# Gated mix of linear attention and a mixer MLP: LayerNorm 1 takes its sums from TensorE and ScalarE, and loads, readers and the last chunk are reordered

## The chip, the core and the metric

The kernel runs on one core of a Trainium2 chip. A core has five engines, each with its own in-order queue of instructions: TensorE (PE in the profile) for matrix products, with weight loads shown apart as PEld; VectorE (DVE) and ScalarE (ACT) for elementwise work; GpSimd (POOL); and SyncE (SP), which here only issues DMA transfers. Products land in PSUM, everything else lives in SBUF. The metric is the device time of one execution, in microseconds (us), as the median of several runs.

## The reference

One input `x` of 2048 rows by 640 columns (bf16) goes through two branches, which a gate mixes row by row.

```python
g = sigmoid((x * gate_w).sum(-1))                 # one gate value for each row

# branch A: linear attention, 32 heads of 20 columns
q, k, v = split(x @ wqkv)
phi = lambda t: where(t > 0, t + 1, exp(t)) + 1e-6
kv  = sum over rows of phi(k)^T v ;  z = sum over rows of phi(k)     # for each head
a   = (phi(q) kv / (phi(q) z + 1e-6)) @ wo

# branch B: mixer MLP
h  = gelu(layernorm(x) @ w1)                      # LayerNorm 1
hs = (four column groups of h, shifted by 1, -1, 2, -2 rows) @ w2
x1 = x + hs
b  = x1 + gelu(layernorm(x1) @ w3) @ w4           # LayerNorm 2

out = g * a + (1 - g) * b
```

A LayerNorm here needs, for each row, the mean and the variance over 640 columns, and no weights.

## The kernel before

The 2048 rows are 16 chunks of 128. The order of all instructions is written out by hand, engine by engine; there is no scheduler. Four PSUM tiles `PP[0..3]` of 128 x 1024 fp32 are handed out by `alloc` and given back by `release`, first in, first out. TensorE waits where a tile that it is given has not yet been read by its last reader.

The stages, by the span of the profiled execution:

- **Start** (to 11 us). `x` is loaded in natural layout (`x_sb`) and, transposed by DMA, as `xT`. Chunks 0 to 2 are transposed on TensorE instead (`x_tr`, L295) and copied out of PSUM by two VectorE copies (L297, L298). The K weights come in five pieces on ScalarE's DMA queue, followed there by the Q weights `wq` (L176); all other loads are on SyncE's queue in program order. Column 640 of the K weights is the gate vector (L305), so that the K product of a chunk also gives the gate's row sums in PSUM column 640.
- **K stage** (11 to 45 us). For each chunk `c`: ten matmuls (`k_mm`, L262) into a PSUM tile; then `k_post`, which calls `phi`: Exp on ScalarE (L256), a min and add on VectorE in SBUF (L257), and a `scalar_tensor_tensor` on VectorE that reads the product in PSUM again (L258). Then a one-column Exp of the gate column on ScalarE (`ey`, L267), and only then `release`. One step of G = x^T phi(K) for chunk c-3 follows on TensorE (`g_unit`, L272, two matmuls), and from chunk 5 on one task of LayerNorm 1.
- **LayerNorm 1 tasks** (`ln1_tasks`): for a chunk two `bn_stats` (L210, L213) and a `bn_aggr` (L214) on VectorE give mean and variance; for each pair of chunks GpSimd makes the reciprocal root by `pow` (L218, L219); VectorE applies it (`ln1_apply`, L226), and SyncE transposes the result into `lnxT` by DMA (L228). In the Q stage three tasks are taken for each Q step.
- **Q stage** (45 to 85 us). Ten Q steps of ten matmuls (L369), each with `phi` over 1024 columns, and five or six G steps behind each; the column sums `z` are made after steps 2 and 4 (`z_rows`, `z_cols`). Then the remaining G steps, the gate (L388 to L390), and four VectorE copies that pack the last 32 columns of each group of `w1` into `w1x` (L396).
- **w1, attention matrices** (85 to 112 us, L404 and others), **w2** (112 to 134 us, L537), **w3 and w4 with the mix** (134 us to the end: L552, L578, L616, L610). The very last chunk is done in two column parts, 512 and 128 columns of one PSUM tile (L610), each with its final VectorE operation (L588) and its output DMA.

Of the kernel before, what the change touches and what calls it, by code (L numbers as in the profile page):

```python
# [16 lines left out]
def kernel(  # L17
# [27 lines left out]
    KW = D + 1  # L45
# [65 lines left out]
    ey = sb("ey", NCH, F32)  # L111
# [64 lines left out]
    aq.dma_start(wq, rows(A_wqkv, 0, D))  # L176
    sp.dma_start(wv, rows(A_wqkv, 2 * D, 3 * D))
    sp.dma_start(w1, rows(B_w1, 0, D))
# [6 lines left out]

    nc.gpsimd.memset(ones32[:], 1.0)
# [36 lines left out]

    def ln1_apply(c):
        lx = lnxs[c % NLX]
        nc.vector.tensor_scalar(lx[:], x_sb[:, c, :], mv1[:, c, 0:1], rs1[:, c:c + 1],  # L226
                                op0=ALU.subtract, op1=ALU.mult)
# [25 lines left out]
    def phi(dst, src, n):  # L253
        e = eb[ecnt[0] % NE]
        ecnt[0] += 1
        act(e[:, 0:n], src, ACT.Exp)  # L256
        nc.vector.tensor_scalar(e[:, 0:n], e[:, 0:n], 1.0, 1e-6, op0=ALU.min, op1=ALU.add)  # L257
# [7 lines left out]
    def k_post(c, p):  # L265
        phi(pk[:, c, :], PP[p][:, 0:D], D)
        act(ey[:, c:c + 1], PP[p][:, D:D + 1], ACT.Exp, scale=-1.0)  # L267
# [25 lines left out]
    def x_tr(c, b):  # L293
# [3 lines left out]
        nc.vector.tensor_copy(xT[:, 0:2, c * P:(c + 1) * P], v[:, 0:2])  # L297
        nc.vector.tensor_copy(xT[:, 2:5, c * P:(c + 1) * P], v[:, 2:5])  # L298
# [5 lines left out]
    for dc in range(DC):  # L304
        nc.vector.tensor_copy(wkg[:, dc, D:D + 1], tb[1][:, dc:dc + 1])  # L305
# [360 lines left out]
```

## Time and profile before

| what | value |
|---|---|
| time, median of 3 runs | 281.55 us (281.39 to 282.06) |
| the profiled execution's own time | 280.44 us |
| its span in the profile | 278.7 us |
| granted TensorE clock | 0.998 of full speed |
| busy PE, DVE, ACT, POOL | 95%, 48%, 35%, 11% of the span |
| DMA | 23.95 MB, mean 86 GB/s |

The span is what the profiler sees from the first to the last instruction; 1.7 us of the profiled execution lie around it. In rows of the timeline the columns are start (us from the span's start), duration, engine, line, operation, output <- input, count, and in brackets how long the engine stood idle before it and which instruction ended that wait. Two consecutive matmuls overlap in the records, so the distance from start to start, not the duration, is what a matmul costs TensorE.

### The profile page before, as it was taken

The numbers are of one execution on the slowest core, as the hardware profiler recorded it, in microseconds if no ns is written. First come the engines' busy times: TensorE is split into PE (matmuls) and PEld (weight loads), VectorE is DVE, ScalarE is ACT, GpSimd is POOL, SyncE is SP. The second block draws the span as 40 slices with busy tenths as digits, with TensorE's granted clock in tenths as the row PEclk, the third lists the DMA queues.
The fourth block names the chain that finished last, engine by engine and source line by source line (L and its number), as shares of the span: only waits on it lengthen the run. The fifth ranks groups of instructions, "written<-read, shape, count | busy, mean of one in ns | idle before, by whom it ended". The sixth has DMA issues, their size and how long they took to land.

```text
span 278.7 us, 4206 instructions
## 1 busy us (share of the span) xinstructions
PE 263.7 (95%) x1698; PEld 135.9 (49%) x1698; DVE 132.7 (48%) x266; ACT 98.4 (35%) x129; POOL 31.9 (11%) x98
## 2 busy tenths in 40 slices
PE   5868888999998999999999999999999999999994
PEld 2434444555553644555444445555544444555552
DVE  2257778989974606599990012432310001233242
ACT  1133433333324476133598550220215445022020
POOL 4000101111210000044685000000000000000000
PEclk9999999999999999999999999999999999999999
DMA  7999960412452026995274100010010000001001
GB/s 205 260 274 282 271 146 2 87 24 45 81 46 52 0 51 210 356 289 79 51 115 95 23 2 24 24 49 24 26 47 0 0 2 0 24 26 47 27 24 48
DMA packets 42119, 23.95 MB, mean 86 GB/s; under 512 B 30963, under 2 KB 41331, under 8 KB 42099
## 3 DMA queue, kind: packets, MB, share of 16 engines
q1 hardware_dynamic: 40690, 22.04, 33.6%
q10 hardware_dynamic: 1376, 1.64, 1.9%
q8 instruction: 13, 0.21, 0.3%
q14 instruction: 8, 0.06, 0.1%
q0 software_dynamic: 32, 0.00, 0.0%
HBM read 12.86 MB, written 3.44 MB: 58 GB/s over the span
## 4 chain that ended last, share of the span: by engine, by line
PE 81%; DVE 10%; ACT 5%; issue 1%; DMA 1%; POOL 0%; DVEq 0%
PE pp L616 19%; PE pp L552 19%; PE pp L404 8%; PE pp L578 8%; PE pp L537 8%; PE pp L369 7%; DVE RPK L258 5%; ACT eb L256 4%; PE pp L272 4%; DVE eb L257 2%; PE pp L561 2%; PE pp L610 1%; PE pp L262 1%; DMA RXH<-in_A_x_dram 1%; PE pp L601 1%
## 5 line engine op out<-in xcount | busy, mean ns | idle before, releaser
L616 PE MATMUL pp<-RB,RXH 128*128 128x512 bf16 (+1 forms) x390 | 54.4, 299 | 0.0
L552 PE MATMUL pp<-lnxT,RA 128*128 128x512 bf16 x240 | 52.1, 379 | 0.0
L616 PEld LDWEIGHTS <-RXH 128*128 128x128 bf16 x390 | 29.7, 98 | 24.2 <-issue 2.1
L552 PEld LDWEIGHTS <-RA 128*128 128x128 bf16 x240 | 23.4, 98 | 28.1
L554 ACT ACTIVATE RXH<-pp 128x1024 bf16<-128x1024 f32 x24 | 24.2, 1019 | 26.7 <-PE pp L552 26.7
L581 ACT ACTIVATE RXH<-pp,g_all 128x640 f32<-128x640 f32 x16 | 12.7, 794 | 54.9 <-PE pp L578 54.9
L256 ACT ACTIVATE eb<-pp 128x640 bf16<-128x640 f32 (+1 forms) x26 | 21.4, 823 | 24.6 <-PE pp L369 20.0
L262 PE MATMUL pp<-RA,RXT 128*128 128x512 bf16 (+1 forms) x160 | 24.3, 299 | 6.1 <-ACT ey L267 5.3
L272 PE MATMUL pp<-RPK,RXH 128*128 128x512 bf16 (+1 forms) x160 | 25.6, 299 | 1.5 <-DVE RPK L258 1.1
L583 DVE SCALAR_TENSOR_TENSOR RPK<-RPK,omg,RXH 128x640 f32<-128x640 f32 x8 | 7.1, 884 | 36.5 <-ACT RXH L581 36.5
L369 PE MATMUL pp<-RXT,RA 128*128 128x512 bf16 x100 | 23.2, 379 | 0.5 <-ACT ey L267 0.3
L578 PE MATMUL pp<-Mp,pqT 128*128 128x512 bf16 (+1 forms) x160 | 23.1, 299 | 0.0
L537 PE MATMUL pp<-w,RXH 128*128 128x512 bf16 (+1 forms) x160 | 21.9, 299 | 0.0
L262 PEld LDWEIGHTS <-RXT 128*128 128x128 bf16 x160 | 12.7, 97 | 17.2 <-issue 7.0
L583 DVE SCALAR_TENSOR_TENSOR RXT<-RXT,omg,RXH 128x640 f32<-128x640 f32 x8 | 7.1, 884 | 24.6 <-ACT RXH L581 24.6
L272 PEld LDWEIGHTS <-RXH 128*128 128x128 bf16 x160 | 12.8, 98 | 12.2 <-issue 1.7
L218 POOL TENSOR_SCALAR ve<-mv 128x1 f32<-128x1 f32 (+1 forms) x24 | 5.6, 235 | 113.0 <-DVE mv L214 112.4
L404 PE MATMUL pp<-lnxT,RB 128*128 128x512 bf16 x80 | 18.3, 379 | 0.0
L578 PEld LDWEIGHTS <-pqT 128*128 128x128 bf16 x160 | 12.2, 98 | 10.0 <-issue 0.8
L537 PEld LDWEIGHTS <-RXH 128*128 128x128 bf16 x160 | 12.3, 98 | 9.6
L588 DVE SCALAR_TENSOR_TENSOR RXH<-pp,omg,RPK 128x640 bf16<-128x640 f32 (+2 forms) x9 | 7.3, 809 | 20.1 <-PE pp L616 17.2
L588 DVE SCALAR_TENSOR_TENSOR RXH<-pp,omg,RXT 128x640 bf16<-128x640 f32 x8 | 7.1, 884 | 19.8 <-PE pp L616 19.8
(102 smaller groups left out, 247.4 us busy)
## 6 DMA issues: line engine op xcount, KB each, us to landing
out_dram<-RXH SPq DMA_DIRECT2D x15, 160.0 KB, 1.8
RA<-in_B_w_dram SPq DMA_DIRECT2D x5, 432.0 KB, 6.9
RXH<-in_A_x_dram SPq DMA_DIRECT2D x2, 640.0 KB, 5.1
RB<-in_B_w_dram SPq DMA_DIRECT2D x1, 1120.0 KB
RB<-in_B_w_dram SPq DMA_DIRECT2D x1, 960.0 KB, 13.0
RA<-in_A_wqkv_dram ACTq DMA_DIRECT2D x5, 160.0 KB, 4.1
RA<-in_A_wqkv_dram ACTq DMA_DIRECT2D x1, 800.0 KB, 8.5
RA<-in_A_wqkv_dram SPq DMA_DIRECT2D x1, 800.0 KB, 6.8
```

The lines of the kernel that those rows point to most:

```text
L256: act(e[:, 0:n], src, ACT.Exp)
L262: mm(PP[p][:, n0:n1], lhsT=xT[:, dc, c * P:(c + 1) * P], rhs=wkg[:, dc, n0:n1], start=(dc == 0), stop=(dc == DC - 1))
L272: mm(PP[p][:, n0:n1], lhsT=x_sb[:, c, i * P:(i + 1) * P], rhs=pk[:, c, n0:n1], start=(c == 0), stop=(c == NCH - 1))
L369: mm(PP[p][:, tt * 512:(tt + 1) * 512], lhsT=wqp[:, dc, j], rhs=xT[:, dc, t0:t0 + 512], start=(dc == 0), stop=(dc == DC - 1))
L404: mm(PP[p][:, tt * 512:(tt + 1) * 512], lhsT=lh, rhs=lnxT[:, dc, t0:t0 + 512], start=(dc == 0), stop=(dc == DC - 1))
L537: mm(PP[p][:, n0:n1], lhsT=hsT[:, fc, 2 + c * P:2 + (c + 1) * P], rhs=w2[:, fc, n0:n1], start=(fc == 0), stop=(fc == DC - 1))
L552: mm(PP[p][:, k * 512:(k + 1) * 512], lhsT=w3[:, dc, (fc + k) * P:(fc + k + 1) * P], rhs=lnxT[:, dc, t * 512:(t + 1) * 512], start=(dc == ...
L554: act(h2T[:, t % 2, fc:fc + 2, :], PP[p][:].rearrange("p (k s) -> p k s", k=2), ACT.Gelu_apprx_tanh)
L578: mm(PP[p][:, n0:n1], lhsT=pqT[:, j, c * P:(c + 1) * P], rhs=Mp[:, j, n0:n1], start=(j == 0), stop=(j == DC - 1))
L583: nc.vector.scalar_tensor_tensor(x1(c), x1(c), omg[:, c:c + 1], ga, op0=ALU.mult, op1=ALU.add)
L588: nc.vector.scalar_tensor_tensor(oc[:, n0:n1], PP[p][:, n0:n1], omg[:, c:c + 1], x1(c)[:, n0:n1], op0=ALU.mult, op1=ALU.add)
L616: mm(PP[p][:, n0:n1], lhsT=h2T[:, k, fc, cc], rhs=w4[:, fc, n0:n1], start=False, stop=(fc == NF - 1))
```

## The change

- The K weights get a second extra column, of ones (`KW = D + 2`), set by GpSimd. PSUM column 641 of a chunk's K product is then the row sum of `x`.
- In `k_post`, ScalarE copies both extra columns (gate and row sum) to `ym` directly behind the Exp of `phi`; the Exp for the gate is taken once for all chunks behind the Q stage.
- LayerNorm 1: ScalarE squares a chunk with a running sum (`ln1_sq`); after each fourth chunk GpSimd makes mean, variance and reciprocal root for four chunks. `bn_stats` and `bn_aggr` of LayerNorm 1 are gone. One `ln1_sq` is taken at every second chunk from 4 on in the K stage and at each Q step; `ln1_apply` is taken at chunks 12 to 15, at Q steps 3, 4, 7 and 8 (two each), and four behind the Q stage.
- Loads: the K weight pieces 0, 1, 2, 4 stay on ScalarE's queue, piece 3 goes to SyncE's behind the first three chunks; the transposed loads are cut 1, 1, 2, 2, 3, 4 chunks instead of 1, 2, 2, 4, 4; `wq` goes to SyncE's queue behind all of `x`, then `w1`, then `wv`.
- The `w1x` packing moves from VectorE behind the Q stage to GpSimd, ahead of all its LayerNorm work.
- `x_tr`: the copy out of PSUM is split between VectorE (3 of 5 blocks) and ScalarE (2 of 5). Its place among the first K matmuls is moved.
- `z_rows`: a small transpose comes ahead of the column sums instead of behind.
- The last chunk's two column parts get a PSUM tile each.

```diff
-    KW = D + 1
+    KW = D + 2
...
-    for dc in range(DC):
-        aq.dma_start(wkg[:, dc, 0:D], A_wqkv[dc * P:(dc + 1) * P, D:2 * D])
+    def load_wk(q, dc):
+        q.dma_start(wkg[:, dc, 0:D], A_wqkv[dc * P:(dc + 1) * P, D:2 * D])
+    for dc in (0, 1, 2, 4):
+        load_wk(aq, dc)
     load_x(0, 1)
     load_x(1, 2)
     load_x(2, 3)
+    load_wk(sp, 3)
     load_xT(3, 4)
+    load_xT(4, 5)
     load_x(3, 4)
-    load_xT(4, 6)
+    load_xT(5, 7)
     load_x(4, 6)
...
-    aq.dma_start(wq, rows(A_wqkv, 0, D))
+    sp.dma_start(wq, rows(A_wqkv, 0, D))
+    sp.dma_start(w1, rows(B_w1, 0, D))
     sp.dma_start(wv, rows(A_wqkv, 2 * D, 3 * D))
-    sp.dma_start(w1, rows(B_w1, 0, D))
...
+    for dc in range(DC):
+        nc.gpsimd.memset(wkg[:, dc, D + 1:D + 2], 1.0)
...
+    for g in range(4):
+        nc.gpsimd.tensor_copy(w1x4[:, :, g, :], w1g[:, :, g, P:CG])
...
+    def ln1_sq(c):
+        act(junk[:], x_sb[:, c, :], ACT.Square, accum_out=sq[:, c:c + 1])
+        if c % 4 == 3:
+            g = slice(c - 3, c + 1)
+            nc.gpsimd.tensor_scalar(me[:, g], ym[:, g, 1], 1.0 / D, None, op0=ALU.mult)
+            nc.gpsimd.tensor_tensor(ve[:, g], me[:, g], me[:, g], op=ALU.mult)
+            nc.gpsimd.tensor_scalar(sq[:, g], sq[:, g], 1.0 / D, EPS, op0=ALU.mult, op1=ALU.add)
+            nc.gpsimd.tensor_tensor(ve[:, g], sq[:, g], ve[:, g], op=ALU.subtract)
+            nc.gpsimd.tensor_tensor(rs1[:, g], ve[:, g], nhalf[:], op=ALU.pow)
...
-    def phi(dst, src, n):
+    def phi(dst, src, n, extra=None):
         e = eb[ecnt[0] % NE]
         ecnt[0] += 1
         act(e[:, 0:n], src, ACT.Exp)
+        if extra is not None:
+            act(extra[0], extra[1], ACT.Copy)
...
     def k_post(c, p):
-        phi(pk[:, c, :], PP[p][:, 0:D], D)
-        act(ey[:, c:c + 1], PP[p][:, D:D + 1], ACT.Exp, scale=-1.0)
+        phi(pk[:, c, :], PP[p][:, 0:D], D, (ym[:, c, :], PP[p][:, D:D + 2]))
         release(p)
...
-        nc.vector.tensor_copy(xT[:, 0:2, c * P:(c + 1) * P], v[:, 0:2])
-        nc.vector.tensor_copy(xT[:, 2:5, c * P:(c + 1) * P], v[:, 2:5])
+        nc.vector.tensor_copy(xT[:, 0:3, c * P:(c + 1) * P], v[:, 0:3])
+        act(xT[:, 3:5, c * P:(c + 1) * P], v[:, 3:5], ACT.Copy)
...
         g_unit(0, c - 3)
-        if c >= 5:
-            pop(ln1_tasks, 1)
+        if c % 2 == 0:
+            pop(ln1_s)
+        if c >= 12:
+            pop(ln1_a)
...
-            pop(ln1_tasks, 3)
+            pop(ln1_s)
+            if n_ in (3, 4, 7, 8):
+                pop(ln1_a, 2)
...
-    for g in range(4):
-        nc.vector.tensor_copy(w1x4[:, :, g, :], w1g[:, :, g, P:CG])
...
         ps = [alloc(), alloc()]
+        if last:
+            ps.append(alloc())
...
-                for (n0, n1) in COLS:
+                for (p, (n0, n1)) in zip((ps[1], ps[2]), COLS):
```

What this does to the order on the engines is shown at three places. In these rows `pp` is a PSUM tile, `eb` a buffer of Exp results, `RXH` holds `x_sb`, `RXT` holds `xT`, `RPK` holds phi(K), `RB` holds `w1`; `[waits DVE_49]` means that the instruction waits for a count of finished VectorE instructions. Line numbers of the changed kernel are up to 16 higher than before.

ScalarE in the K stage before the change, chunks 3 to 5:

```order
L256 ACTIVATE eb_70<-pp_114 128x640 [waits PE_49]
L267 ACTIVATE ey<-pp_114 128x1 [waits DVE_49]
L256 ACTIVATE eb_71<-pp_112 128x640 [waits PE_49]
L267 ACTIVATE ey<-pp_112 128x1 [waits DVE_49]
L256 ACTIVATE eb_72<-pp_113 128x640 [waits PE_49]
L267 ACTIVATE ey<-pp_113 128x1 [waits DVE_49]
```

ScalarE in the K stage after the change, chunks 3 to 5:

```order
L268 ACTIVATE eb_70<-pp_116 128x640 [waits DVE_49,PE_49]
L270 ACTIVATE ym<-pp_116 128x2
L268 ACTIVATE eb_71<-pp_114 128x640 [waits DVE_49,PE_49]
L270 ACTIVATE ym<-pp_114 128x2
L239 ACTIVATE junk,sq<-RXH 128x640 [waits DMAHW1_49]
L268 ACTIVATE eb_72<-pp_115 128x640 [waits DVE_49,PE_49]
L270 ACTIVATE ym<-pp_115 128x2
```

The small reader of the extra columns no longer waits for VectorE; the Exp now waits for VectorE itself, since one of three `eb` buffers is used again, and the first Square stands between chunks 4 and 5.

GpSimd behind its set-up work, before the change (the first LayerNorm pair):

```order
L201 MEMSET RXH 128x5x4
L202 MEMSET RXH 128x5x4
L218 TENSOR_SCALAR ve<-mv_94 128x2 [waits DVE_49]
L219 TENSOR_TENSOR rs_97<-ve,nhalf 128x2 [waits Pool_49]
L218 TENSOR_SCALAR ve<-mv_94 128x2 [waits DVE_49]
```

The same place after the change:

```order
L211 MEMSET RXH 128x5x4
L212 MEMSET RXH 128x5x4
L216 COPY w1x<-RB 128x5x32 [waits DMAHW4_49]
L216 COPY w1x<-RB 128x5x32 x3
L242 TENSOR_SCALAR me<-ym 128x4 [waits Activation_49]
L243 TENSOR_TENSOR ve<-me 128x4 [waits Pool_49]
L244 TENSOR_SCALAR sq<-sq 128x4 [waits Activation_49]
L245 TENSOR_TENSOR ve<-sq,ve 128x4 [waits Pool_49]
L246 TENSOR_TENSOR rs_99<-ve,nhalf 128x4 [waits Pool_49]
```

The four copies wait for the DMA that brings `w1`, and the first four chunks' LayerNorm values stand behind them in GpSimd's queue.

VectorE at chunks 12 to 14 of the K stage, after the change:

```order
L272 SCALAR_TENSOR_TENSOR RPK<-pp_116,eb_70 128x640 [waits DVE_49,PE_49,Activation_49]
L250 TENSOR_SCALAR lnxs_73<-RXH,me,rs_99 128x640 [waits DMAHW1_49,Pool_49]
L271 TENSOR_SCALAR eb_71<-eb_71 128x640 [waits Activation_49]
L272 SCALAR_TENSOR_TENSOR RPK<-pp_114,eb_71 128x640 [waits DVE_49,PE_49,Activation_49]
L250 TENSOR_SCALAR lnxs_74<-RXH,me,rs_99 128x640 [waits DMAHW3_49]
L271 TENSOR_SCALAR eb_72<-eb_72 128x640 [waits Activation_49]
```

The first `ln1_apply` (L250) waits for GpSimd, and the second half of `phi` of chunks 13, 14 and 15 stands behind it on VectorE.

More of the change, by code (lines that the diff above doesn't have):

```diff
@@ L334, in z_rows @@
     def z_rows():
+        p = alloc()
+        nc.tensor.transpose(PP[p][:, 0:64].bitcast(BF16), mask4[:], ident[:])
+        act(E4[:], PP[p][:, 0:64].bitcast(BF16), ACT.Copy)
+        release(p)
         p = alloc()
@@ L382 @@
         g_unit(*gq.pop(0))
-        pop(ln1_tasks, 1)
-    while ln1_tasks:
-        pop(ln1_tasks)
-    nc.vector.tensor_scalar(g_all[:], ey[:], 1.0, None, op0=ALU.add)
+    assert not ln1_s
+    pop(ln1_a, 4)
+    assert not ln1_a
+    act(g_all[:], ym[:, :, 0], ACT.Exp, scale=-1.0)
+    nc.vector.tensor_scalar(g_all[:], g_all[:], 1.0, None, op0=ALU.add)
     nc.vector.reciprocal(g_all[:], g_all[:])
     nc.vector.tensor_scalar(omg[:], g_all[:], -1.0, 1.0, op0=ALU.mult, op1=ALU.add)
-    w1g = w1.rearrange("p k (g c) -> p k g c", c=CG)
-    w1x4 = w1x.rearrange("p k (g c) -> p k g c", g=4)
-    for g in range(4):
-        nc.vector.tensor_copy(w1x4[:, :, g, :], w1g[:, :, g, P:CG])
     def w1_unit(half, fc):
@@ L600, in w4_units @@
                 q = slice(FT * k, FT * (k + 1))
-                mm(PP[ps[k]][:, n0:n1], lhsT=h2x[q, cc], rhs=w4[q, NF, n0:n1], start=True, stop=False,
+                p = ps[2] if last and k == 1 and n0 else ps[k]
+                mm(PP[p][:, n0:n1], lhsT=h2x[q, cc], rhs=w4[q, NF, n0:n1], start=True, stop=False,
                    tile_position=(FT * k, 0))
```

44 lines of the change are left out of this document (16 added, 28 removed).

## The prediction

> **What bounds the kernel now.** I read the busy shares first, then the busy time by stage, then the waits in order of size, then the timeline at the places that the waits name. The stages are marked by the first Exp (11.2), the first G step alone (45.0), the first w1 product (85.1).
>
> ```profile
> PE 263.7 (95%) x1698; PEld 135.9 (49%) x1698; DVE 132.7 (48%) x266; ACT 98.4 (35%) x129; POOL 31.9 (11%) x98
> 11.20:45.00 33.80, 26.71 (x174) 14.30 (x173) 23.62 (x48) 12.21 (x32) 1.92 (x4) 1.00 0.90 221
> 45.00:85.10 40.10, 39.16 (x263) 21.44 (x262) 35.53 (x84) 14.45 (x18) 6.01 (x12) 1.00 0.31 51
> 133.90:278.70 144.80, 141.02 (x889) 70.98 (x886) 41.01 (x67) 48.17 (x54) 13.48 (x40) 1.00 0.13 31
> ```
>
> The reader is to see that TensorE (first busy column behind the length) is the bound everywhere but in the K stage, where it is busy 26.7 of 33.8 us, VectorE 23.6 and ScalarE 12.2. No engine is full there, so a chain of waits must set the pace.
>
> ```profile
> ACT ey L267 <- DVE RPK L258: 21.6, 16, 1.7
> PE pp L262 <- ACT ey L267: 5.3, 12, 1.7
> PE pp L272 <- DVE RPK L258: 1.1, 1, 1.1
> PE pp L404 <- DVE w1x L396: 0.8, 1, 0.8
> PE pp L610 <- DVE RXH L588: 0.8, 1, 0.8
> ```
>
> Each of 16 chunks makes ScalarE wait, 21.6 us in all, for the last VectorE operation of `phi` before the one-column `ey`, and TensorE waits 12 times for that `ey`. The timeline shows the ring.
>
> ```profile
> 17.65 1.52 PE L262 MATMUL pp<-RA,RXT 128*128 128x512 bf16 x10 [0.29 <-ACT ey L267]
> 18.23 0.33 DVE L257 TENSOR_SCALAR eb<-eb 128x640 bf16<-128x640 bf16 x1 [0.83 <-ACT eb L256]
> 18.66 0.82 DVE L258 SCALAR_TENSOR_TENSOR RPK<-pp,eb 128x640 bf16<-128x640 f32 x1
> 19.01 0.43 PE L272 MATMUL pp<-RPK,RXH 128*128 128x512 bf16 x2
> 19.51 0.17 ACT L267 ACTIVATE ey<-pp 128x1 f32<-128x1 f32 x1 [1.32 <-DVE RPK L258]
> 19.74 1.52 PE L262 MATMUL pp<-RA,RXT 128*128 128x512 bf16 x10 [0.29 <-ACT ey L267]
> ```
>
> Exp (what VectorE waits for at 18.23), min, product, `ey`, and only then the next Exp: the next chunk's matmuls come 19.74 - 17.65 = 2.09 us later. ScalarE's queue is in order, so `ey`, not its 0.17 us, holds back the next Exp. TensorE itself needs 19.01 - 17.65 = 1.36 us for ten K matmuls, and 0.27 for a G step (8 G matmuls, four steps, in 46.08 - 45.00 below): 1.63 us a chunk.
>
> **The change: the K stage.** The copy of both extra columns now stands directly behind Exp and waits for nothing on VectorE, so the ring is cut. What remains for a chunk: TensorE 1.63; VectorE 0.43 from min to product and 0.82 for the product, 1.27 with the gaps, 1.70 where an `ln1_apply` of 0.43 is added; ScalarE 0.70 + 0.17, and a Square at every second chunk. Square has no row; the nearest are Exp from PSUM at 0.70 and the 640-column ACTIVATE below at 0.92. I take 0.80, since it reads SBUF like the dearer one but without per-row operands: two chunks then cost ScalarE 2 x 0.87 + 0.80 = 2.54, against TensorE's 3.26. TensorE becomes the bound. `bn_stats` leaving VectorE is worth nothing on top: VectorE had 10 us idle here. The wider K matmul adds one column of 641 and is neglected.
>
> ```profile
> 11.21 0.70 ACT L256 ACTIVATE eb<-pp 128x640 bf16<-128x640 f32 x1 [4.56 <-PE pp L262]
> 15.56 1.52 PE L262 MATMUL pp<-RA,RXT 128*128 128x512 bf16 x10 [1.66 <-ACT ey L267]
> 41.03 2.32 PE L369 MATMUL pp<-RXT,RA 128*128 128x512 bf16 x10 [0.29 <-ACT ey L267]
> 45.00 1.25 PE L272 MATMUL pp<-RPK,RXH 128*128 128x512 bf16 x8 [1.11 <-DVE RPK L258]
> 46.08 2.32 PE L369 MATMUL pp<-RXT,RA 128*128 128x512 bf16 x10
> 48.24 1.52 PE L272 MATMUL pp<-RPK,RXH 128*128 128x512 bf16 x10
> L518 ACT ACTIVATE lnxs<-RPK,nb,rs 128x640 bf16<-128x640 f32 x8 | 7.3, 915 | 1.8 <-POOL nb L222 1.3 <-DMA lnxT<-lnxs 0.5
> L226 DVE TENSOR_SCALAR lnxs<-RXH,mv,rs 128x640 bf16<-128x640 bf16 x16 | 6.2, 431 | 1.1 <-POOL rs L219 1.1
> ```
>
> With the first Exp at 11.21 as before, chunk 4's matmuls (15.56) need the tile of chunk 1: 11.21 + 0.74, then two rounds of 1.26 on VectorE, is 14.5. Twelve chunks at 1.63 put the first Q step at 14.5 + 19.6 = 34.1 (before 41.03). A Q step is 48.24 - 46.08 = 2.16, six G steps 1.63, so the second Q step starts at 37.9 (before 46.08): **8.2 us** gained if nothing new waits. The waits of 1.66 and 1.11 in these rows are in that.
>
> **The new wait.** GpSimd's four `w1x` copies wait for `w1`; the LayerNorm values of chunks 0 to 3 are queued behind them; `ln1_apply(0)` waits for those, and behind it on VectorE stand `phi` of chunks 13 to 15, for which TensorE waits.
>
> ```profile
> 22.39 0.51 SPq L177 DMA_DIRECT2D RA<-in_A_wqkv_dram  x1
> RA<-in_A_wqkv_dram SPq DMA_DIRECT2D x1, 800.0 KB, 6.8
> 22.93 0.52 SPq L178 DMA_DIRECT2D RB<-in_B_w_dram  x1
> RB<-in_B_w_dram SPq DMA_DIRECT2D x1, 800.0 KB, 9.7
> 30.66 0.25 POOL L218 TENSOR_SCALAR ve<-mv 128x2 f32<-128x2 f32 x1 [25.94 <-DVE mv L214]
> 30.98 0.72 POOL L219 TENSOR_TENSOR rs<-ve,nhalf 128x2 f32<-128x2 f32 x1
> L191 POOL TENSOR_SCALAR_AFFINE_SELECT bmask<-bmask 128x120 f32<-128x120 f32 x1 | 0.3, 332 | 0.1
> ```
>
> Before, `wv` landed at 22.39 + 6.8 = 29.2 and `w1` behind it at 22.93 + 9.7 = 32.6. In the new order one 800 KB matrix fewer lies ahead of `w1` (`wq` moves from ahead of most of `x` to just ahead of it, `wv` behind it), which these two rows price at 3.4 us: `w1` lands between 29.2 and 32.6. I take 30.0, near the lower end, since what counts ahead of it is bytes. GpSimd then needs four copies at about 0.35 (nearest row: 0.33 for 120 columns, these have 160) and five small operations, four at 0.31 from start to start and one `pow` of 0.75: 3.4 us, so `ln1_apply(0)` starts at a = 33.4. `phi(12)` is done at 31.0, so VectorE stands for 2.4 us. The first Q step needs `phi(13)`'s tile, at a + 1.7 = 35.1 instead of 34.1; the G step of chunk 15 needs `phi(15)` at a + 5.1 = 38.5, where TensorE would be at 37.8. TensorE loses 1.0 + 0.7 = **1.7 us**; generally a - 31.7 where that is positive. At the ends: 0.9 for `w1` at 29.2, nothing for 28.3 or earlier, 4.3 for 32.6.
>
> By the Trainium skill ("SBUF — State Buffer", Who interferes with whom), VectorE's two-port modes and GpSimd lock each other out for a whole instruction, which speaks against four copies on GpSimd beside `phi`. The copies would wait out at most a min of 0.33 each, an estimate of 1.3 us more on the loss; no row of this trace has such a pair, and I leave it to the range.
>
> **Loads and start.** `wq` now comes behind `x`, where `wv` was: by 29.2 at the latest, against the first Q step at 34.1, so it costs nothing; each microsecond past 34.1 would be lost in full. The transposed `x` for chunks 12 to 15 came at
>
> ```profile
> 17.12 4.60 SPq L155 DMA_TRANSPOSE RXT<-in_A_x_dram  x1
> RXT<-in_A_x_dram SPq DMA_TRANSPOSE x1, 8.2
> L297 DVE COPY RXT<-pp 128x256 bf16<-128x256 bf16 x3 | 0.9, 292 | 5.2 <-PE pp L295 5.2
> L298 DVE COPY RXT<-pp 128x384 bf16<-128x384 bf16 x3 | 1.0, 347 | 0.0
> L345 ACT ACTIVATE E<-pp 128x128 bf16<-128x128 bf16 x1 | 0.3, 273 | 0.0
> ```
>
> 25.3 and is needed at 14.5 + 8 x 1.63 = 27.5: enough, with 2.2 us to spare even at the old time. The split of `x_tr`'s copies is not parallel: ScalarE's part waits for VectorE's, so 0.35 + about 0.38 (between 0.27 for 128 columns and 0.70 for 640) replaces 0.29 + 0.27 on the chain to the gate column, up to 0.2 for each of two chunks; against it the third transpose no longer follows so many K matmuls, and the weights come 0.8 MB freer. I take 0, with 0.4 both ways.
>
> By the Trainium skill ("PSUM — Partial Sum Buffer", PSUM bank collisions raise a hardware error), two engines must not touch one bank at once, reads included. That is why `ey` had to wait for a reader of other columns, the 21.6 us above, and why the split copies run one behind the other; the trace agrees with it.
>
> **Q stage and end.**
>
> ```profile
> 53.21 1.27 PE L339 MATMUL pp<-RPK,ones 128*32 128x512 bf16 x32
> 85.14 2.33 PE L404 MATMUL pp<-lnxT,w1x 128*128 128x512 bf16 x10 [0.80 <-DVE w1x L396]
> 274.07 0.75 DVE L588 SCALAR_TENSOR_TENSOR RXH<-pp,omg,RPK 128x512 bf16<-128x512 f32 x1 [1.92 <-PE pp L610]
> 274.87 0.89 PE L610 MATMUL pp<-RB,RXH 128*128 128x128 bf16 x13 [0.84 <-DVE RXH L588]
> 275.80 0.35 DVE L588 SCALAR_TENSOR_TENSOR RXH<-pp,omg,RPK 128x128 bf16<-128x128 f32 x1 [0.98 <-PE pp L610]
> ```
>
> From 46.08 to 85.14 TensorE has nine Q steps (19.4), 61 G steps (16.5) and the column sums (1.3 and 0.4): 37.6 of 39.1 us. The 0.80 for `w1x`, with the 0.16 of overlap that a stop costs, goes to GpSimd 50 us earlier: **1.0 us**. The other 0.5 stays, since the third Q step's tile is still the one that the fourth gets, whatever the order of `z_rows`. VectorE, now 1.66 plus at most 0.86 in a Q step of 3.52, gives no more, and ScalarE has 1.02 + 0.80 and at times 0.70. From 85 us on nothing changes until the last chunk: the 128-column part need not wait for the 512-column part's reader, so 0.84 + 0.16 goes: **1.0 us**. VectorE still takes 0.75 before the last 0.35, which then ends at 275.2 instead of 276.15, and the output DMAs follow.
>
> **Sum**, on the profiled execution's 280.44 us (span 278.7): 8.2 - 1.7 + 1.0 + 1.0 = 8.5 less, 271.9. The median of the runs is 281.55, 1.1 above that execution, so the forecast for a median is **273.0 us**.
>
> **Rivals.**
> - *The new wait does not bite* (`w1` by 28.3): 1.7 more is gained, 271.3. For it: with a matrix fewer ahead, the last loads of `x` can also be issued earlier, which the two landings don't count. Against: both bounds above lie later. Chance 0.18.
> - *It bites in full* (`w1` at 32.6 again, or copies that are locked out): 4.3 lost instead of 1.7, 275.6. For it: the one landing that the trace has. Chance 0.16.
> - *A transposed load becomes the bound* of the quicker K stage: it must come over 2.2 us later than before, for instance because SyncE now issues six transposes; each costs its delay once; with 3 us, 276.0. Against: 0.8 MB fewer ahead of it. Chance 0.06.
> - *The ring stays*, with the Exp's own new wait on VectorE in place of `ey`'s, at 2.09 us a chunk: only 1.0 + 1.0 + the 1.1 of the first chunks remain, 278.5. Against: three `eb` buffers make that a wait for three chunks back. Chance 0.06.
> - *Slower:* Square with its running sum is far dearer than any row. The K stage then runs at half of 1.74 + s for a Square of s us, and is slower than 2.09 from s = 2.4; a Q step of 3.52 breaks at about s = 2.3. At s = 3.5 the K stage loses 6 and the Q stage about 10 us: 296. It needs 2.6 times the longest 640-column row. Chance 0.04.
>
> **How the numbers follow.** The forecast has 0.50. Its own range is 271.5 to 274.5 (`w1` between 29.2 and about 31, the start 0.4 both ways). The range for 8 in 10 takes in both sides of the new wait: 270.6 to 276.2. A change below 0.3%, 0.8 us, cannot be told from none. All cases but the last are faster; leaving something for what I have not seen, 0.93 faster, 0.03 within 0.3%, 0.04 slower.
>
> **What would show it.** In the changed profile: K matmuls of consecutive chunks 1.63 apart and no wait of ScalarE for VectorE in the K stage; Square near 0.8; one wait of VectorE on GpSimd of about 2.4 us near 31 us, and TensorE waiting for VectorE about there; the second Q step near 39.6; no wait before the w1 products or in the last chunk. The forecast is wrong if chunks stay 2 us apart, if ScalarE is busy beyond TensorE's pace, or if a K matmul waits for a DMA.

## The result: 272.22 us, 9.6 us less, and the profile after

| | before | after |
|---|---|---|
| median of the runs | 281.81 us (281.39 to 283.11) | 272.22 us (272.13 to 272.27) |
| profiled execution, span | 280.44 us, 278.7 us | 272.18 us, 270.5 us |

The ratio of the times is 0.9652, 95% interval 0.9619 to 0.9685. The profiled execution lost 8.26 us; the forecast was 8.5 for it and 273.0 us for a median.

The busy shares of the changed kernel, from its page:

```profile
PE 262.2 (97%) x1698; PEld 136.5 (50%) x1698; DVE 116.0 (43%) x211; ACT 110.7 (41%) x165; POOL 32.9 (12%) x111
```

Its busy time by stage, from the first Exp (11.6) to the lone G step (38.5), and on to the first w1 product (77.7). Behind the length stand PE, PEld, DVE, ACT and POOL, then the granted clock, the DMA share and GB/s.

```profile
11.60:38.50 26.90, 24.98 (x175) 13.89 (x173) 19.08 (x36) 17.48 (x46) 3.52 (x11) 1.00 1.11 270
38.50:77.70 39.20, 38.90 (x264) 21.58 (x264) 23.16 (x41) 19.51 (x35) 5.11 (x13) 1.00 0.33 52
```

The K stage is 26.9 us long instead of 33.8, and TensorE is now busy in 93% of it instead of 79%. The timeline of the changed kernel (start, duration, engine, line, operation, count, idle time before and what ended it) shows the cut ring, with a Square beside it.

```profile
16.55 1.53 PE L276 MATMUL pp<-RA,RXT 128*128 128x512 bf16 x10
17.08 0.17 ACT L270 ACTIVATE ym<-pp 128x2 f32<-128x2 f32 x1
17.13 0.74 ACT L239 ACTIVATE junk<-RXH 128x640 bf16<-128x640 bf16 x1
17.76 0.20 ACT L239 ACTIVATION_READ_ACCUMULATOR junk<-RXH 128x1 f32 x1
18.11 0.70 ACT L268 ACTIVATE eb<-pp 128x640 bf16<-128x640 f32 x1 [0.15 <-PE pp L276]
18.18 1.53 PE L276 MATMUL pp<-RA,RXT 128*128 128x512 bf16 x10
```

Chunks are 18.18 - 16.55 = 1.63 us apart instead of 2.09, and ScalarE waits for TensorE, no longer for VectorE. The price stands in its timeline around the end of the K stage and the first w1 product:

```profile
29.90 1.20 POOL L216 COPY w1x<-RB 128x160 bf16<-128x160 bf16 x4 [24.95 <-DMA RB<-in_B_w_dram]
30.29 0.37 DVE L271 TENSOR_SCALAR eb<-eb 128x640 bf16<-128x640 bf16 x1 [0.35 <-ACT eb L268]
32.24 1.05 POOL L246 TENSOR_TENSOR rs<-ve,nhalf 128x4 f32<-128x4 f32 x1
33.33 0.45 DVE L250 TENSOR_SCALAR lnxs<-RXH,me,rs 128x640 bf16<-128x640 bf16 x1 [1.71 <-POOL rs L246]
35.02 2.32 PE L384 MATMUL pp<-RXT,RA 128*128 128x512 bf16 x10 [0.33 <-DVE RPK L272]
38.52 1.25 PE L285 MATMUL pp<-RPK,RXH 128*128 128x512 bf16 x8 [0.64 <-DVE RPK L272]
39.60 2.32 PE L384 MATMUL pp<-RXT,RA 128*128 128x512 bf16 x10
77.70 2.32 PE L417 MATMUL pp<-lnxT,w1x 128*128 128x512 bf16 x10
```

GpSimd stands until `w1` is there at 29.90, VectorE stands 1.71 us for GpSimd (the forecast had about 2.4), TensorE 0.33 and 0.64 for VectorE. The landmarks divide the gain of 8.2 us between the two spans. The second Q step starts at 39.60 instead of 46.08: 6.5. From there to the first w1 product it is 38.10 instead of 39.06: 1.0. From there to the end it is 192.8 instead of 193.6: 0.8.

### The profile page after: what moved, and what is told of

Its sections match the earlier page's. It is cut to its first block, busy times and chain, and to the rows that moved or that the text cites. A ratio compares the mean times of both kernels' runs of the same rounds, so it can differ in the third digit from the quotient of the medians.

```text
span 270.5 us, 4220 instructions
## 1 busy us (share of the span) xinstructions
PE 262.2 (97%) x1698; PEld 136.5 (50%) x1698; DVE 116.0 (43%) x211; ACT 110.7 (41%) x165; POOL 32.9 (12%) x111
## 4 chain that ended last, share of the span: by engine, by line
PE 84%; SPq 6%; DMA 4%; DVE 2%; POOL 1%; issue 1%; ACT 0%; DVEq 0%
PE pp L632 20%; PE pp L565 19%; PE pp L417 8%; PE pp L384 8%; PE pp L591 8%; PE pp L550 8%; PE pp L285 6%; SPq L157 5%; DMA RB<-in_B_w_dram 3%; PE pp L574 2%; PE pp L617 1%; SPq L154 1%; PE pp L626 1%; DMA RA<-in_A_wqkv_dram 1%; PE pp L581 1%; PE pp L451 1%
## 5 line engine op out<-in xcount | busy, mean ns | idle before, releaser
L565 PEld LDWEIGHTS <-RA 128*128 128x128 bf16 x240 | 23.4, 98 | 28.1
L276 PE MATMUL pp<-RA,RXT 128*128 128x512 bf16 (+1 forms) x160 | 25.0, 307 | 0.8 <-DVE RPK L272 0.8
L271 DVE TENSOR_SCALAR eb<-eb 128x640 bf16<-128x640 bf16 (+1 forms) x26 | 9.5, 365 | 19.4 <-ACT eb L268 19.4
L591 PEld LDWEIGHTS <-pqT 128*128 128x128 bf16 x160 | 12.2, 98 | 10.0 <-issue 0.8
L384 PEld LDWEIGHTS <-RA 128*128 128x128 bf16 x100 | 11.2, 117 | 9.6 <-issue 0.7
```

The source lines that it names most:

```text
L276: mm(PP[p][:, n0:n1], lhsT=xT[:, dc, c * P:(c + 1) * P], rhs=wkg[:, dc, n0:n1], start=(dc == 0), stop=(dc == DC - 1))
L384: mm(PP[p][:, tt * 512:(tt + 1) * 512], lhsT=wqp[:, dc, j], rhs=xT[:, dc, t0:t0 + 512], start=(dc == 0), stop=(dc == DC - 1))
L565: mm(PP[p][:, k * 512:(k + 1) * 512], lhsT=w3[:, dc, (fc + k) * P:(fc + k + 1) * P], rhs=lnxT[:, dc, t * 512:(t + 1) * 512], start=(dc == ...
L591: mm(PP[p][:, n0:n1], lhsT=pqT[:, j, c * P:(c + 1) * P], rhs=Mp[:, j, n0:n1], start=(j == 0), stop=(j == DC - 1))
```

## The experiments

Each kernel was timed beside runs of the kernel before, whose median on the chips used was 282.0 to 282.7 us. Intervals are 95% intervals of the ratio to it.

**The change once more**, to have its own spread beside the next three.

> The changed kernel once more, as the base of this group of runs: 272.2 us. No theory expects anything else.

Measured: 272.62 us (272.31 to 273.23), ratio 0.9653 (0.9625 to 0.9680). Its profile differs from the first one at the start, which is taken up below: its first Exp came at 13.50 us instead of 11.64. With that the new wait is gone from it.

```profile
30.30 1.22 POOL L216 COPY w1x<-RB 128x160 bf16<-128x160 bf16 x4 [25.36 <-DMA RB<-in_B_w_dram]
40.17 2.10 PE L384 MATMUL pp<-RXT,RA 128*128 128x512 bf16 x9
```

`w1` landed 0.40 later than in the first profile, VectorE still stood 0.3 us for GpSimd, but TensorE did not wait for VectorE at the start of the Q stage. Here the late K products alone set the second Q step. So whether the new wait bites, and how far, hangs on how early the start is.

**The ring cut alone.** The kernel before, with one edit: the one-column Exp of the gate directly behind the Exp of `phi`. `bn_stats` stay on VectorE.

```diff
     def phi(dst, src, n, extra=None):
         act(e[:, 0:n], src, ACT.Exp)
+        if extra is not None:
+            act(extra[0], extra[1], ACT.Exp, scale=-1.0)
```

> The kernel before with one edit: the gate column's Exp stands directly behind the Exp of phi. bn_stats stay on VectorE, loads and all else as before. Theory (the ring of Exp, min, product and ey was the K stage's bound, and taking bn_stats off VectorE adds nothing to it): chunks about 1.8 us apart, since VectorE has 1.19 for phi and on average 0.6 for LayerNorm tasks; the second Q step starts near 39 us (46.1 before, 39.6 in the changed kernel), so 7 us are gained of the kernel before: about 274.5. Rival (the sums had to leave VectorE for the K stage to run faster): chunks at 2.0 or more, 279 to 281.

Measured: 274.31 us (273.43 to 274.78), ratio 0.9706 (0.9673 to 0.9739). Its timeline in the K stage, with a `bn_stats` between two `phi`:

```profile
18.48 0.70 ACT L256 ACTIVATE eb<-pp 128x640 bf16<-128x640 f32 x1 [0.87 <-PE pp L264]
18.55 1.53 PE L264 MATMUL pp<-RA,RXT 128*128 128x512 bf16 x10
19.08 0.17 ACT L258 ACTIVATE ey<-pp 128x1 f32<-128x1 f32 x1
20.18 1.52 PE L264 MATMUL pp<-RA,RXT 128*128 128x512 bf16 x9
20.41 0.48 DVE L210 BATCH_NORM_STATS2 bst<-RXH 128x6 f32<-128x320 bf16 x1
```

One moved instruction gives 7.9 of the 9.6 us, and 20.18 - 18.55 = 1.63 us a chunk (1.8 were expected) with VectorE still doing all of LayerNorm 1. So the row-sum column and the Squares did not buy the pace of the K stage. The second Q step of this profile starts at 39.09, no later than in the two profiles of the changed kernel (39.60 and 40.17). What the changed kernel has over this one lies behind it: from the second Q step to the end it is 232.6 us here, as before the change, and 230.9 in the first profile after.

**The ring put back.** The changed kernel with the copy of the two columns behind `phi` again.

```diff
-        phi(pk[:, c, :], PP[p][:, 0:D], D, (ym[:, c, :], PP[p][:, D:D + 2]))
+        phi(pk[:, c, :], PP[p][:, 0:D], D)
+        act(ym[:, c, :], PP[p][:, D:D + 2], ACT.Copy)
```

> The changed kernel with one edit undone: the copy of the two extra columns stands behind phi again, as ey did. Theory: chunks 2.09 us apart again, but GpSimd's values come in time then, so the second Q step starts near 45 (39.6 in the changed kernel): 5 to 6 us lost, 277.5 to 278.5. Rival (most of the gain comes from the sums on ScalarE and the loads): 272 to 274.

Measured: 286.17 us (285.85 to 286.83), ratio 1.0138 (1.0104 to 1.0171): worse than before the change, and 8 us worse than expected. Its timeline shows why:

```profile
20.66 0.17 ACT L281 ACTIVATE ym<-pp 128x2 f32<-128x2 f32 x1 [1.32 <-DVE RPK L272]
22.75 0.17 ACT L281 ACTIVATE ym<-pp 128x2 f32<-128x2 f32 x1 [1.32 <-DVE RPK L272]
22.81 0.73 ACT L239 ACTIVATE junk<-RXH 128x640 bf16<-128x640 bf16 x1
23.53 0.69 ACT L268 ACTIVATE eb<-pp 128x640 bf16<-128x640 f32 x1
25.55 0.17 ACT L281 ACTIVATE ym<-pp 128x2 f32<-128x2 f32 x1 [1.32 <-DVE RPK L272]
```

The copy waits for VectorE as `ey` did, the Square is queued behind the copy, and the next Exp behind the Square: the ring is 22.75 - 20.66 = 2.09 us without a Square and 25.55 - 22.75 = 2.80 with one. I had counted the ring of the kernel before, which had no Square in it, and a second Q step near 45 us; it came at 51.98. Six of the chunks in the loop carry a Square, which is about 4.3 us of the 8. The first Exp came at 12.36 instead of 11.21, which is 1.1 more, and I had counted on about 1.1 at the first chunks (a second Q step at 45 instead of 46.1) that did not come. The rest, 1.7 us, is TensorE itself behind the loop:

```profile
50.00:60.00 10.00, 9.47 (x45) 4.62 (x46) 4.08 (x6) 5.02 (x9) 1.84 (x5) 0.83 0.09 18
50.47 1.71 PE L286 MATMUL pp<-RPK,RXH 128*128 128x512 bf16 x8 [2.23 <-DVE RPK L272]
51.98 3.58 PE L385 MATMUL pp<-RXT,RA 128*128 128x512 bf16 x10
55.40 1.52 PE L286 MATMUL pp<-RPK,RXH 128*128 128x512 bf16 x10
```

Over these 10 us the granted clock was 0.83. The eight G matmuls behind a wait of 2.23 us took 51.98 - 50.47 = 1.51 us, where in the profile before they took 46.08 - 45.00 = 1.08, and the ten Q matmuls behind them 55.40 - 51.98 = 3.42 instead of 2.16. From 18 to 20 us the clock was granted at 0.50 as well, behind a wait of 1.66, but there ScalarE's copies stayed 2.09 apart and the ring lost nothing. A wait alone does not bring this about: the kernel before had a wait of 1.66 at the same place at a granted clock of 1.00, and in a run below a wait of 2.86 stands ahead of ten Q matmuls of the usual 2.32. What rule it follows is open.

**The new wait taken away.** The changed kernel with GpSimd's four `w1x` copies behind the first LayerNorm batch instead of ahead of it.

```diff
-    for g in range(4):
-        nc.gpsimd.tensor_copy(w1x4[:, :, g, :], w1g[:, :, g, P:CG])
...
             nc.gpsimd.tensor_tensor(rs1[:, g], ve[:, g], nhalf[:], op=ALU.pow)
+        if c == 3:
+            for q in range(4):
+                nc.gpsimd.tensor_copy(w1x4[:, :, q, :], w1g[:, :, q, P:CG])
```

> The changed kernel with the four w1x copies on GpSimd placed behind the LayerNorm values of chunks 0 to 3 instead of ahead of them. Theory (GpSimd's wait for w1 holds back ln1_apply(0), and through it phi of chunks 13 to 15): VectorE's wait of 1.7 us near 32 us is gone, TensorE's waits of 0.33 and 0.64 behind it too, the first Q step at 34.5 and the second near 38.3: 1.3 us gained, 270.9. Rival (TensorE waits there for another reason, or loses the same time later): 272.2.

Measured: 271.32 us (271.07 to 272.33), ratio 0.9611 (0.9580 to 0.9642), 1.3 under the changed kernel's 272.62 on the same chip. In its profile TensorE does not wait for VectorE at the start of the Q stage. But neither does it in the repeated run's profile, and these two differ only as their starts do: first Exp at 13.06 and 13.50, second Q step at 39.73 and 40.17, time 272.33 and 272.74. So the 1.3 us is a difference of medians that this pair of profiles does not explain; what the wait costs is read from the runs below that have it.

**The new wait made longer.** The changed kernel with `wv` loaded ahead of `w1`.

```diff
-    sp.dma_start(w1, rows(B_w1, 0, D))
     sp.dma_start(wv, rows(A_wqkv, 2 * D, 3 * D))
+    sp.dma_start(w1, rows(B_w1, 0, D))
```

> The changed kernel with one edit: wv is loaded ahead of w1, so that w1 comes some 3.9 us later (its landing was 29.84 in the changed kernel). Theory (GpSimd's w1x copies, queued ahead of the first batch of LayerNorm 1, wait for w1, and the wait passes to TensorE at the first Q step): w1 lands near 33.7, the first apply starts near 37.2 instead of 33.33, TensorE's waits in front of the second chunk of work of the Q stage grow from 0.97 to about 4, second Q step near 43, time about 276.0 (275.0 to 277.0; a late start of the K stage takes some of it back, since the wait then overlaps it). Rival (the landing of w1 doesn't set the first Q steps): 272.6, second Q step near 39.6.

Measured: 275.76 us (274.86 to 276.38), ratio 0.9770 (0.9720 to 0.9820). The rows that matter in its timeline:

```profile
33.02 1.11 POOL L216 COPY w1x<-RB 128x160 bf16<-128x160 bf16 x4 [28.07 <-DMA RB<-in_B_w_dram]
38.06 2.32 PE L384 MATMUL pp<-RXT,RA 128*128 128x512 bf16 x10 [2.86 <-DVE RPK L272]
42.65 2.32 PE L384 MATMUL pp<-RXT,RA 128*128 128x512 bf16 x10
```

`w1` came 3.1 us later than in the first profile after (the forecast was 3.9), and the second Q step 42.65 - 39.60 = 3.05 later.

**The start filled, with the wait left in.** The changed kernel with four products on zeros added, which keep TensorE busy in its gaps before 7 us (why, comes below).

```diff
-    for _ in range(5):
+    for _ in range(6):
         mm(PP[3][:, 512:1024], lhsT=warm[:, 0:P], rhs=warm[:], start=True, stop=True)
...
     x_tr(0, 0)
+    fill(2)
     nc.tensor.transpose(tb[1][:, 0:DC], g5[0:DC, :], ident[0:DC, 0:DC])
...
+    fill(1)
     x_tr(1, 1)
```

> The changed kernel with the four products on zeros that fill TensorE's gaps at the start, the w1x copies where the change put them. Theory (with the copies ahead of LayerNorm 1, w1's landing at 29.8 to 30 sets the first Q steps, whatever the start): the full rate by 6 us and the K products done earlier, but the waits of TensorE at the Q stage's start grow by what the start gains; first Q step near 35.0 and second near 39.6 as in the changed kernel; time 272.2 (271.9 to 272.6), no difference from it. Rival (the wait for w1 is only a part, and the start comes through): 271.8 or less, as the fillers were worth 0.8 in the version without this wait.

Measured: 273.26 us (272.93 to 273.45), ratio 0.9690 (0.9661 to 0.9718), 1 us over the expected value. Its timeline:

```profile
30.92 1.11 POOL L216 COPY w1x<-RB 128x160 bf16<-128x160 bf16 x4 [25.96 <-DMA RB<-in_B_w_dram]
35.96 2.32 PE L390 MATMUL pp<-RXT,RA 128*128 128x512 bf16 x10 [1.71 <-DVE RPK L272]
40.54 2.32 PE L390 MATMUL pp<-RXT,RA 128*128 128x512 bf16 x10
```

The K products were done earlier, and TensorE's wait grew to 1.71. `w1` came 1.02 later than in the first profile, which I had not allowed for, and the second Q step 0.94 later; why `w1` lands between 29.90 and 30.92 with the same order of loads is open. Together with the next run there are four profiles in which TensorE waits here, and the distance from `w1` to the second Q step is one and the same: 39.60 - 29.90 = 9.70, 40.23 - 30.53 = 9.70, 40.54 - 30.92 = 9.62, 42.65 - 33.02 = 9.63. Where the wait bites, `w1`'s landing sets the start of the Q stage, and the K stage does not.

**The last chunk in one pair again.** The changed kernel with the third `alloc` taken out.

```diff
         ps = [alloc(), alloc()]
-        if last:
-            ps.append(alloc())
...
-                for (p, (n0, n1)) in zip((ps[1], ps[2]), COLS):
+                for (n0, n1) in COLS:
```

> The changed kernel with one edit: the last chunk's two column parts in one PSUM pair again, as before the change. Theory: TensorE waits again some 0.84 us for VectorE's read of the first part; time 272.6 + 0.8 = 273.4 (272.9 to 273.9), and from the first w1 product to the end 193.6 instead of 192.8. Rival (the wait of the last chunk is worth nothing, the 0.76 between the profiles came from elsewhere): 272.6, and no wait of TensorE in the last 6 us.

Measured: 273.44 us (272.82 to 273.67), ratio 0.9682 (0.9641 to 0.9722). The rows of its timeline for the wait at the start of the Q stage and for the last chunk:

```profile
30.53 1.11 POOL L216 COPY w1x<-RB 128x160 bf16<-128x160 bf16 x4 [25.57 <-DMA RB<-in_B_w_dram]
40.23 2.32 PE L384 MATMUL pp<-RXT,RA 128*128 128x512 bf16 x10
268.05 0.89 PE L623 MATMUL pp<-RB,RXH 128*128 128x128 bf16 x13 [0.84 <-DVE RXH L601]
```

The wait of 0.84 is back, and from the first w1 product (78.3) to the end (271.9) it is 193.6 us, as before the change. The interval of the ratio alone would not tell 0.8 us; the rows do.

**`w1x` on VectorE again.** The changed kernel with the four copies at their old place behind the gate.

```diff
-        nc.gpsimd.tensor_copy(w1x4[:, :, g, :], w1g[:, :, g, P:CG])
...
     nc.vector.tensor_scalar(omg[:], g_all[:], -1.0, 1.0, op0=ALU.mult, op1=ALU.add)
+    for g in range(4):
+        nc.vector.tensor_copy(w1x4[:, :, g, :], w1g[:, :, g, P:CG])
```

> The changed kernel with one edit: the four w1x copies are VectorE's again, at their old place behind the Q stage. Theory: the wait for w1 at the Q stage's start goes (as in the version with the copies behind the first LayerNorm batch, 271.32), and TensorE's wait for the copies in front of the w1x products comes back (0.8 in the run with the ring cut alone, 1.0 between the profiles of before and after): from the second Q step to the first w1x or w1 product 39.06 instead of 38.10, time 271.3 + 0.9 = 272.2 (271.8 to 272.9), no difference from the changed kernel (272.62). Rival (the 0.96 of the Q stage came from something else of the change): 271.3, and no wait of TensorE for w1x.

Measured: 274.02 us (273.56 to 276.35), ratio 0.9745 (0.9691 to 0.9800), 1.8 over the expected value. Its timeline behind the Q stage:

```profile
77.65 0.21 ACT L403 ACTIVATE g_all<-ym 128x16 f32<-128x16 f32 x1
77.89 0.17 DVE L404 TENSOR_SCALAR g_all<-g_all 128x16 f32<-128x16 f32 x1 [0.84 <-ACT g_all L403]
78.47 0.53 DVE L408 COPY w1x<-RB 128x160 bf16<-128x160 bf16 x4
79.06 1.25 PE L417 MATMUL pp<-lnxT,w1x 128*128 128x512 bf16 x5 [2.05 <-DVE w1x L408]
```

The first Q steps were free again, as expected. But the change also made the gate one Exp on ScalarE behind the last G column's copy, VectorE waits 0.84 for it, and the copies stand behind: TensorE waits 2.05 instead of 0.80. In the changed kernel the move of the copies is therefore worth more than the 1.0 between the profiles; with the gate's batch Exp, it has to go along.

**What the start does.** In the repeated run of the change, the weight loads of TensorE, one for each K matmul (a pair of matmuls, 512 and 130 columns wide, has two), read:

```profile
11.65 0.26 PEld L276 LDWEIGHTS <-RXT 128*128 128x128 bf16 x2 [0.27 <-issue]
12.15 0.92 PEld L276 LDWEIGHTS <-RXT 128*128 128x128 bf16 x7 [0.24 <-issue]
```

A pair of loads came about every 0.53 us up to 12.15; then seven loads took 0.92, about 0.27 a pair, twice as fast, though the granted clock reads 1.00 in both stretches. In the profile of the kernel before, this moment lay near 6 us; in the first profile after near 8.6; in the other seven executions with such a start between 8.4 and 12.2. By the Trainium skill ("TensorE: Matmul & The Clock Gate", What's actually happening) TensorE runs at half rate until a free-running window of some 3.4 us was busy throughout. The trace agrees with the half rate; that unbroken work opens it, the next runs tried. They start from the kernel with the copies behind the first LayerNorm batch, so that the start can reach the end. First the four products on zeros as above:

> The version with the w1x copies behind the first LayerNorm batch (271.32 in its run), with four more products on zeros that keep TensorE busy while it waits for x0 and for the first copies. In the profiles so far the K products of the start run in pairs 0.53 us apart, half of the later rate, until some moment that differs between executions (about 6 us in the kernel before, 8.6 in the changed one, 10.2, 11.1 and 12.2 in three others), with the granted clock shown as 1.00 throughout. Theory (TensorE gets its full rate only after a stretch of unbroken work, and the gaps at the start decide when): the full rate is reached by 8 us in each execution, first Exp near 11.2 instead of 13.06, and without the w1 wait all of it reaches the end: 269.6 (269.0 to 270.4). Rival 1 (the slow pairs come from the loads that arrive at the same time): pairs as before, 271.3. Rival 2 (the transposed loads bound the K stage once it starts earlier): full rate early, but new waits of TensorE for DMA, about 270.8 to 271.3.

Measured: 270.54 us (270.27 to 270.61), ratio 0.9581 (0.9541 to 0.9620), 0.9 over the expected value and just outside its range. The second Q step:

```profile
37.66 2.32 PE L391 MATMUL pp<-RXT,RA 128*128 128x512 bf16 x10
```

This kernel and the one of 273.26 us above differ in the place of the `w1x` copies alone, and both start early (first Exp at 10.99 and 11.20). So the pair prices the new wait: 2.7 us by medians, taken on two chips, and 40.54 - 37.66 = 2.88 by the second Q step, of which 0.21 is the start.

Then the transposes of the first three chunks in PSUM pairs of their own, one copy each, and three products on zeros:

```diff
-        nc.vector.tensor_copy(xT[:, 0:3, c * P:(c + 1) * P], v[:, 0:3])
-        act(xT[:, 3:5, c * P:(c + 1) * P], v[:, 3:5], ACT.Copy)
+        if c == 1:
+            act(xT[:, :, c * P:(c + 1) * P], v, ACT.Copy)
+        else:
+            nc.vector.tensor_copy(xT[:, :, c * P:(c + 1) * P], v)
...
+    x_tr(0, 3)
+    fill(1)
+    x_tr(1, 2)
...
+    x_tr(2, 1)
+    fill(1)
```

> The version with the w1x copies behind the first LayerNorm batch, with two edits at the start: the transposes of the first three x chunks go to three PSUM pairs of their own, each copied out by one instruction (chunks 0 and 2 by VectorE, chunk 1 by ScalarE), the gate column's transpose to a fourth; and three more products on zeros fill TensorE's gaps. Theory (TensorE waits 0.86 for ScalarE's copy of x0 and 0.51 for VectorE because these share a PSUM pair, and its rate depends on the gaps): both waits go, first K product near 6.0 instead of 6.5 to 6.9, first Exp near 10.5, time 268.9 (268.2 to 270.0). Rival (loads of the K weights or the transposed loads bound it): waits of TensorE for DMA instead, 270 to 271.3.

Measured: 269.95 us (269.36 to 272.05), ratio 0.9578 (0.9536 to 0.9620); two of its six runs were near 272, for a reason that no profile shows, so that the medians alone do not part it from the 270.54. The K products of the start, and the first Exp, in the filled kernel and then in this one:

```profile
7.64 5.22 PE L277 MATMUL pp<-RA,RXT 128*128 128x512 bf16 x35
10.99 0.70 ACT L269 ACTIVATE eb<-pp 128x640 bf16<-128x640 f32 x1 [2.30 <-PE pp L277]
```

```profile
6.34 5.61 PE L277 MATMUL pp<-RA,RXT 128*128 128x512 bf16 x39
10.08 0.70 ACT L269 ACTIVATE eb<-pp 128x640 bf16<-128x640 f32 x1 [3.83 <-PE pp L277]
```

Without fillers the same kernel had its first Exp at 13.06. With them the K products go at full rate from the first one on, in all five profiles of kernels that have them. The gain by medians (0.8, then 0.6) is less than the profiles' 2.1 and 0.9, since the profile without fillers was one with a late full rate (and the slowest of its four runs). Whether it is unbroken work or simply more work that brings the full rate was not separated. The loads did not hold it back: no K matmul waits for a DMA.

**Chunk by chunk.** The same, with the first K products ordered by chunk instead of by input block.

```diff
-    for dc in range(2, DC):
-        for c in range(3):
-            k_mm(c, c, dc)
-            if dc == DC - 1:
-                k_post(c, c)
+    for c in range(3):
+        for dc in range(DC):
+            k_mm(c, c, dc)
+        k_post(c, c)
```

> The version with the first three x chunks transposed into pairs of their own and TensorE's gaps filled (269.95), with one more edit: the K products of the first three chunks are issued chunk by chunk instead of input block by input block. Theory (the three Exps come together at the end of the shared stretch, so that TensorE waits 0.76 and 0.21 for VectorE in front of chunks 3 and 4): first Exp at 6.3 + 1.4 + 0.2 = 8.0 instead of some 10.1, both waits go, time 269.95 - 0.95 = 269.0 (268.4 to 269.7). Rival 1 (the last K weight blocks aren't there by then): TensorE waits for DMA in the first chunk, 269.5 to 270. Rival 2 (the ring's length, not the start, holds the K stage, or a transposed load does): another wait in its place, 270.

Measured: **268.52 us** (268.47 to 268.95), ratio 0.9526 (0.9498 to 0.9554). In its timeline

```profile
6.85 5.61 PE L277 MATMUL pp<-RA,RXT 128*128 128x512 bf16 x40
8.41 0.70 ACT L269 ACTIVATE eb<-pp 128x640 bf16<-128x640 f32 x1 [1.66 <-PE pp L277]
12.57 1.52 PE L277 MATMUL pp<-RA,RXT 128*128 128x512 bf16 x10
```

the waits of 0.76 and 0.21 ahead of chunk 4 are gone, and TensorE runs from 6.85 us through the K stage with no wait. This version beats both kernels, the changed one by 3.7 us (272.22), or 4.1 by its repeated run (272.62).

**Room on ScalarE.** The last one, with each Square done twice, the second into a column that nothing reads.

> The best version so far (268.52) with each Square of LayerNorm 1 done twice, the second into a column that nothing reads: 0.73 + 0.20 more for ScalarE per Square, 6 of them in the K loop, 10 in the Q stage. Theory (the Square stands beside the ring, not in it; in the K loop ScalarE has 2 x (0.70 + 0.17) + 0.93 = 2.67 of work in two chunks' 3.27, so that a second Square makes 3.60 and ScalarE the bound by 0.33 per two chunks; the Q steps have room): 6 x 0.33 = 2.0 more, 270.5 (269.4 to 271.2). Rival 1 (ScalarE's work in the K loop reaches TensorE in full, as in the run with the ring cut undone): 6 x 0.93 = 5.6 more, 274. Rival 2 (room left, because the Exps run ahead): 268.5 to 269.

Measured: 268.66 us (268.50 to 270.87), ratio 0.9554 (0.9487 to 0.9622): no difference, where 2 us were expected. ScalarE in its K stage:

```profile
14.20 0.70 ACT L271 ACTIVATE eb<-pp 128x640 bf16<-128x640 f32 x1 [0.87 <-PE pp L279]
14.85 0.74 ACT L238 ACTIVATE junk<-RXH 128x640 bf16<-128x640 bf16 x1
15.71 0.74 ACT L239 ACTIVATE junk<-RXH 128x640 bf16<-128x640 bf16 x1
17.47 0.70 ACT L271 ACTIVATE eb<-pp 128x640 bf16<-128x640 f32 x1 [0.28 <-PE pp L279]
```

From Exp to Exp of two chunks it is 17.47 - 14.20 = 3.27, TensorE's pace, with 0.28 idle. I had added up durations and got 3.60. On ScalarE, too, rows overlap: a Square with its accumulator read takes 15.71 - 14.85 = 0.86 of the queue, not 0.93, and Exp and copy together 14.85 - 14.20 = 0.65, not 0.87.

## Why the prediction was right

The likeliest case came, inside its own range, by the steps that it named; three sizes and one addend were off.

- **The ring (8.2).** Right in mechanism and nearly in size: alone it gave 7.9 by medians. That `bn_stats` leaving VectorE is worth nothing on top for the pace is borne out by 1.63 us a chunk with them still there. The start took some of it back: the first Exp came at 11.64, not 11.21.
- **The new wait (1.7).** Right in place and chain: `w1` at 29.90 (taken: 30.0), `ln1_apply(0)` at 33.33 (33.4), first Q step at 35.02 (35.1), the lone G step at 38.52 (38.5). Its price hangs on the start, which the prediction took as fixed. In the first profile TensorE waited 0.97, since the first Exp was 0.4 late; in the repeated run's, with the first Exp 2.3 late, it did not wait. In the filled kernel whose first Exp came at 11.20, as forecast, `ln1_apply(0)` started at 34.27: the rule a - 31.7 gives 2.6, and the pair of filled kernels shows 2.7. The rule that it costs as much as `w1` is late held in the longer wait too: 3.05 for 3.1 us. The second Q step at 39.60 (39.6) owes nothing to the size of the ring's gain: late start and cheaper wait are the same 0.4, and `w1`'s landing sets the step. That `w1` came so near the 30.0 taken is part luck, as it landed anywhere from 29.90 to 30.92 in the five profiles with these loads and the copies in this place.
- **The copies beside `phi`.** From the Trainium skill ("SBUF — State Buffer", Who interferes with whom) I had estimated up to 1.3 us for four copies on GpSimd beside `phi`. The four copies took 1.20 us together, and the min beside them (30.29) stretched from 0.33 to 0.37: none of that price is to be seen here.
- **Loads and start (0, 0.4 both ways).** Right within its bounds in the first profile, but for a reason that I did not have. I priced the copies of `x_tr`, while the largest thing at the start is when TensorE reaches its full rate, which put the first Exp anywhere from 11.64 to 13.50 us among executions with the changed kernel's loads and `x_tr`. The transposed loads did come in time: no K matmul waits for a DMA in any of the profiles.
- **Square (0.80).** Measured 0.73, plus a separate accumulator read of 0.20 that I had not foreseen. It cost nothing beside the ring, and doubled still nothing. The rival that a dear Square makes the kernel slower lacked one condition: the Square hurts at its ordinary price once it stands inside the ring, 2.80 - 2.09 = 0.71 us for each, as the run of 286.17 us showed.
- **Q stage (1.0) and last chunk (1.0).** Measured 0.96 and 0.76; the two runs that undid these edits brought TensorE's waits back. The last chunk's wait of 0.84 was there, without the 0.16 of overlap that I had added to it. The wait of 0.3 in front of the fourth Q step stayed, as said.
- **The median (1.1 above the profiled execution).** This addend failed. The changed kernel's runs lay within 0.14 us of one another and around its profiled execution; the 1.1 did not carry over, which is why the measured median is 0.8 below the forecast. That before's runs scatter with the start, while the wait for `w1` hides such a scatter in the changed kernel, would explain it. The repeated run's profile fits (its first Exp came 1.86 later than in the first profile, its span is only 0.5 longer), but it is argued, not shown, and the spread of 0.9 in the repeated run speaks for other sources as well.

## What to carry to other kernels

An in-order engine that alternates with another one is paced by where the small instruction stands, not by how long it takes: a 0.17 us read moved ahead of a wait was worth 7.9 us, and a Square with its read, 0.86 us of ScalarE's queue, was free beside the ring and cost 0.71 us each time inside it. Before work is queued ahead of other work on a quiet engine, ask when its input lands, since everything behind it, on the engines that wait for it too, then starts by that landing. A start that differs between profiles of the same kernel is worth a look of its own: filling TensorE's gaps, giving the first transposes PSUM tiles of their own and ordering the first products by chunk gave another 2.8 us here, on top of 1.3 for the misplaced copies; with those copies in place, filling the gaps gained nothing (273.26 us).

## What the hardware showed beside this

- TensorE's half rate at the start ended between 6 and 12.2 us in nine executions without fillers, at a granted clock shown as 1.00; with three or four products on zeros in the gaps the K products ran at full rate in all five.
- An ACTIVATE with a running sum is two instructions in the trace, here 0.73 and 0.20 us.
- In the kernel with the ring put back TensorE ran slower twice more, at a granted clock of 0.50 from 18 to 20 us and behind a wait of 2.23 us (1.51 us for matmuls that took 1.08, 3.42 for 2.16). This half rate is seen in the granted clock; the one at the start, shown as 1.00, is not. Whether they are the same mechanism was not tried.
